# A new stored order of all engines for a fused RWKV-6 attention and Fourier-mix block

## The chip, the cores and the metric

The kernel runs on one core of a Trainium2 chip. The metric is the device time of one execution in microseconds (us). Five engines work side by side, each through its own list of instructions, strictly in the order in which the list was written: TensorE (PE, matrix products; its weight loads are listed as PEld), VectorE (DVE), ScalarE (ACT), GpSimd (POOL) and SyncE (SP), which here only issues DMAs. An instruction waits on semaphores until the instructions it depends on have ended; everything behind it on the same engine waits with it.

## The reference

The first half is a linear attention with a state that decays by step; the second mixes its output by a two-dimensional Fourier transform and puts it through a small two-layer network.

```python
# r, k, v, w: (4 batches, 8 heads, 768 steps, 48); u: (8, 48)
for t in range(S):
    cur = einsum('bhd,bhe->bhde', u * k[t], v[t])
    y[t] = einsum('bhd,bhde->bhe', r[t], state + cur)
    state = w[t][..., None] * state + einsum('bhd,bhe->bhde', k[t], v[t])
x = y as (4, 768, 384)
mixed = real(fft over d of (fft over t of x))
u = x + mixed
un = (u - mean) / sqrt(var + 1e-6)             # over the 384
out = u + relu(un @ w_ch1) @ w_ch2              # 384 -> 1536 -> 384
```

## The kernel before

**Tiling.** Each batch's 768 steps are six chunks of 128 steps on the partitions, so there are 24 chunks; the text writes (b, c) for chunk c of batch b. For each chunk four loads of 192 KB bring w, k, r and v (`load_one`, L621, issued at L624 on SP) into rings of seven buffers a name (`NIN`, L482). `attention` (L783) takes the logarithm of w on ScalarE, sums it over the steps by a matmul with a mask (L799; where the variant `sum_two` is taken also one with the other mask, L822), turns the sums into exponentials, multiplies r and k with them into `rkh`, transposes these (on TensorE at L899 or L911, or by a DMA transpose, L889), multiplies them into the score matrix (L922), masks it on VectorE (L932), updates the state (L954 to L963, from v in bf16, `vb`) and forms the output of the chunk (L984, L987). `fold` (L1014) adds and subtracts mirrored columns, and `mix` (L1048) does the Fourier transform as matmuls with cosine and sine tables (L1063 to L1068, then L1107 or L1116), adds, normalizes, transposes (L1203, or by DMA, L1210) and runs the network by halves of a batch: the first layer is 12 groups of three matmuls (L1235) a half, the second three outputs of 12 matmuls (L1254). So the network of batch b is done while the attention of batch b+1 is under way, and the network of the last batch has nothing beside it. The network's weights come by three DMAs from the POOL queue (`weights`, L766; issued at L769 twice for the first matrix and at L774 for the second); the first has to wait for a load of batch 0 (`W_AFTER`, L31).

**Variants.** Many steps have several forms with the same result (`choose`, L168): an eviction or a product on one engine or two, a transpose by TensorE or by DMA. Which form is taken, and which engine does a step that two engines could do, is decided by the numbers that stand in the stored order.

**The order.** `ORDER` (L38) holds, for each of the five engines, the numbers of the operations in the order in which the engine gets them. Nothing is sorted when the kernel is built; `schedule` (L227) walks the five lists with a model of the durations, and out of this come only the PSUM bank of every tile and some extra waits: a reused bank waits for its former tile, and an operation of POOL waits for the last operation of VectorE that the model put ahead of it on the port they share:

```python
for t, (_, i) in zip(o.opens, free):
    t.bank = i
    if bank[i] is not None:
        o.deps |= set(bank[i].ops)
```

The model's price for a load is the `xfer` in `load_one`, 998 ns for every load. Operations 2638 to 2669 are 32 matmuls without any use (`warm`, L1320): they are placed in the TensorE list like others and keep this engine active. The 16 matmuls at L1287 at the start serve the same end.

**What the steps ahead touch.** The list "sp" with the loads, the transposes at L889 and L1210 and the outputs at L1274; the list "pe"; the place of the three weight DMAs in the list "pool"; `load_one`.

Of the kernel before, what the change touches and what calls it, by code (L numbers as in the profile page):

```python
# [65 lines left out]
    "act": (  # L66
# [384 lines left out]
def bass_rwkv6_finch__then__fnet_fourier_mix_kernel(  # L451
# [169 lines left out]
    def load_one(b, c, n):  # L621
        was, g.ctx = g.ctx, ("load", b, c, n)
        i = (b * NC + c) % NIN
# [731 lines left out]
```

## Time and profile before

| | us |
|---|---|
| median of 3 runs | 182.34 (182.21 to 183.43) |
| the profiled execution, its own time | 182.32 |
| its span, first to last instruction | 180.2 |
| TensorE busy | 172.6 |
| VectorE, ScalarE, GpSimd busy | 155.7, 130.2, 111.0 |

The span is what the views of the profile show; 2.1 us of the execution's time lie around it. A busy TensorE is counted from the issue of a matmul to its modelled end, so matmuls that overlap in the pipeline are one stretch; for sums the distance between the starts of two successive matmuls is the better measure. A wait in the profile is put down to whatever released it last. The granted clock of TensorE stands in a row of its own.

### The profile page before, as it was taken

The page shows a single profiled execution, that of the slowest core. Times are in us where ns is not written, and L with a number is a line of the kernel's source. Part 1 is how long each engine was busy: PE and PEld are TensorE (multiplying, and loading weights), DVE is VectorE, ACT ScalarE, POOL GpSimd, SP SyncE. Part 2 cuts the span into 40 slices and gives each one's busy share as a digit, 9 for nine tenths or more (in the row PEclk, how much of TensorE's full clock was granted, in tenths as well). Part 3 has the DMA queues.
Part 4 walks back from the last instruction along what each step waited for, and adds up shares of the span by engine and source line. Part 5 has one row for each costly group of instructions (what it writes and reads, how often), then busy time and mean ns, then how long its engine had stood idle before and what let it go on. Part 6 is the DMA issues. An engine that isn't in the chain of part 4 may idle for free.

```text
span 180.2 us, 4569 instructions
## 1 busy us (share of the span) xinstructions
PE 172.6 (96%) x1704; PEld 113.9 (63%) x1704; DVE 155.7 (86%) x372; ACT 130.2 (72%) x311; POOL 111.0 (62%) x140
## 2 busy tenths in 40 slices
PE   5988899999999999999999999999999999999994
PEld 2455566766666576866676766665666776656663
DVE  7699999779998899999999999799999966882543
ACT  3989979589899686899997994986981754290500
POOL 2437779697464588599899865898988070310000
PEclk9999999999999999999999999999999999999999
DMA  5999998998998989999899999999973213304113
GB/s 118 209 209 204 178 200 169 183 208 163 171 206 173 211 166 241 202 204 210 191 216 187 232 161 210 233 160 196 217 162 51 91 44 63 135 4 100 39 58 131
DMA packets 117303, 29.29 MB, mean 163 GB/s; under 512 B 112545, under 2 KB 117282, under 8 KB 117282
## 3 DMA queue, kind: packets, MB, share of 16 engines
q1 hardware_dynamic: 115698, 26.65, 73.5%
q0 software_dynamic: 1584, 2.36, 7.7%
q8 instruction: 13, 0.21, 0.5%
q14 instruction: 8, 0.07, 0.1%
HBM read 23.59 MB, written 4.72 MB: 157 GB/s over the span
## 4 chain that ended last, share of the span: by engine, by line
PE 78%; DVE 7%; DMA 5%; ACT 4%; SPq 2%; issue 2%; POOL 1%; DVEq 0%; POOLq 0%; ACTq 0%
PE bank L1254 23%; PE bank L1235 23%; PE bank L1107 4%; PE bank L922 3%; PE bank L1063 3%; DMA in_v<-in_v_dram 3%; PE bank L911 3%; PE bank L1321 2%; PE bank L987 2%; DMA in_w<-in_w_dram 2%; PE bank L799 2%; PE bank L984 2%; PE bank L959 2%; SPq L889 1%; DVE ah L932 1%
## 5 line engine op out<-in xcount | busy, mean ns | idle before, releaser
L1254 PE MATMUL bank<-w,ht 128*128 128x384 bf16 (+2 forms) x300 | 52.8, 319 | 0.0
L1235 PE MATMUL bank<-unt,w 128*128 128x384 bf16 x288 | 52.0, 326 | 0.0
L1243 ACT ACTIVATE ht<-bank 128x384 bf16<-128x384 f32 x70 | 31.2, 497 | 13.2 <-PE bank L1235 13.0
L1254 PEld LDWEIGHTS bank<-w,ht 128*128 128x128 bf16 x300 | 27.5, 98 | 15.4
L1235 PEld LDWEIGHTS bank<-unt,w 128*128 128x128 bf16 x288 | 27.0, 98 | 15.7 <-DVE ah L932 0.2
L932 DVE TENSOR_TENSOR ah<-bank,msk 128x512 bf16<-128x512 f32 x42 | 27.4, 682 | 0.2 <-PE bank L922 0.2
L578 POOL TENSOR_TENSOR rkh<-in_k,e 128x384 bf16<-128x384 f32 x19 | 19.0, 1002 | 7.2 <-ACT e L840 4.9
L1263 DVE SCALAR_TENSOR_TENSOR osb<-bank,rstd,uf 128x384 f32<-128x384 f32 (+2 forms) x25 | 14.7, 596 | 9.0 <-PE bank L1254 9.0
L578 POOL TENSOR_TENSOR vtd<-in_v,dc 128x384 f32<-128x384 f32 x22 | 18.1, 830 | 5.7 <-DVE rk L578 4.1
L578 POOL TENSOR_TENSOR rk<-in_r,in_k 128x384 f32<-128x384 f32 x18 | 17.9, 1001 | 0.0
L578 POOL TENSOR_TENSOR rk<-rk,ub 128x384 f32<-128x384 f32 x17 | 16.9, 997 | 0.8 <-DVE rk L578 0.5
L1241 DVE TENSOR_SCALAR ht<-bank 128x384 bf16<-128x384 f32 x26 | 13.7, 547 | 2.9 <-PE bank L1235 2.9
L601 ACT ACTIVATE rkt<-bank 128x512 bf16<-128x512 bf16 (+1 forms) x19 | 14.5, 781 | 1.1 <-PE bank L911 1.1
L592 ACT ACTIVATE lb<-in_w 128x384 bf16<-128x384 f32 x24 | 12.3, 521 | 3.0 <-DMA in_w<-in_w_dram 2.9
L592 ACT ACTIVATE vb<-in_v 128x384 bf16<-128x384 f32 x23 | 11.9, 522 | 2.2 <-DMA in_v<-in_v_dram 2.2
L578 POOL TENSOR_TENSOR xf<-sd 128x384 bf16<-128x384 f32 (+1 forms) x9 | 8.9, 999 | 7.4 <-DVE xf L578 5.0
L871 DVE TENSOR_REDUCE dc<-rk 128x8 f32<-128x384 f32 (+1 forms) x24 | 12.5, 526 | 0.1
L853 DVE TENSOR_TENSOR rkh<-bank,in_r 128x384 bf16<-128x384 f32 x21 | 11.5, 547 | 0.4 <-ACT bank L852 0.4
L998 DVE TENSOR_TENSOR x<-bank,vtd 128x384 f32<-128x384 f32 x21 | 11.4, 549 | 0.2 <-POOL vtd L578 0.2
L826 ACT ACTIVATE e<-bank 128x392 f32<-128x392 f32 (+1 forms) x18 | 8.8, 497 | 3.4 <-PE bank L813 2.6
L852 ACT ACTIVATE bank<-bank 128x384 f32<-128x384 f32 x21 | 10.1, 486 | 1.7 <-PE bank L799 1.6
L987 PE MATMUL bank<-vb,ah 128*128 128x48 bf16 x192 | 11.1, 183 | 0.0
(185 smaller groups left out, 373.2 us busy)
## 6 DMA issues: line engine op xcount, KB each, us to landing
in_w<-in_w_dram SPq DMA_DIRECT2D x24, 192.0 KB, 3.8
in_r<-in_r_dram SPq DMA_DIRECT2D x24, 192.0 KB, 3.8
in_k<-in_k_dram SPq DMA_DIRECT2D x24, 192.0 KB, 3.9
in_v<-in_v_dram SPq DMA_DIRECT2D x24, 192.0 KB, 4.0
out_dram<-osb SPq DMA_DIRECT2D x23, 192.0 KB, 2.8
w<-in_moe_w_ch_dram POOLq DMA_DIRECT2D x2, 576.0 KB, 8.6
w<-in_moe_w_ch_dram POOLq DMA_DIRECT2D x1, 1152.0 KB, 11.1
out_dram<-osb SPq DMA_DIRECT2D x1, 128.0 KB, 1.7
```

The source lines that it names most:

```text
L578: return lambda e: e.tensor_tensor(out=o, in0=a, in1=b, op=f)
L592: return lambda e: e.activation(o, a, f, **kw)
L601: {"act": lambda e: e.activation(o(), i(), ACTF.Copy), "dve": lambda e: e.tensor_copy(out=o(), in_=i())}, **kw)
L853: op("dve", v_1(DM), lambda e: e.tensor_tensor(out=rh[:, :, 0:D], in0=ps(tce)[:, 0:DM].rearrange("t (h d) -> t h d", d=D), in1=rt[:, :, :] ...
L871: op("dve", v_1(H * m), lambda e: e.tensor_reduce(out=dc[:, :], in_=rku[:, :, 0:m], axis=mybir.AxisListType.X, op=ALU.add), r=[("RK", i2)] ...
L932: masked[n].append(op("dve", v_1(512), lambda e: e.tensor_tensor(out=ah[:, x:H:2, :], in0=ps(bk)[:, :].rearrange("p (h t) -> p h t", t=128 ...
L987: ins = e.matmul(ps(ty)[:, D * h:D * h + D], ah[:, h, :], vb[:, h, :], start=first and not ype, stop=True, skip_group_check=True)
L1235: ins = e.matmul(ps(t)[:, 0:384], W1[:, m, 256 * (j // 2) + j % 2:256 * (j // 2) + 256:2], unt[:, :, m, :], start=(m == 0), stop=(m == NM ...
L1241: {"dve": lambda e, j=j, t=t, ht=ht: e.tensor_scalar(out=ht[:, j, :], in0=ps(t)[:, 0:384], scalar1=su, scalar2=0.0, op0=ALU.mult, op1=ALU. ...
L1243: "act": lambda e, j=j, t=t, ht=ht: e.activation(ht[:, j, :], ps(t)[:, 0:384], ACTF.Relu, scale=su)},
L1254: ins = e.matmul(ps(t)[:, 0:hi - lo], ht[:, j, 128 * x:128 * x + 128], W2[:, j, lo:hi], start=(j == 0), stop=(j == NJ - 1))
L1263: op("dve", v_1(hi - lo) + 64, lambda e: e.scalar_tensor_tensor(out=o[:, lo:hi], in0=ps(t)[:, 0:hi - lo], scalar=rstd[:, kb:kb + 1], in1=u ...
```

## The change

All five lists of `ORDER` are replaced, and the model's price of a load becomes 1040 ns in batch 2 and 1075 ns in batch 3. Compared by the operations' numbers, the two orders differ in this:

- 1418 operations stand in both. 73 are dropped and 78 are new, all of them other forms of the same steps: one DMA transpose of `rkh` fewer (chunk (3, 1) is transposed on TensorE now, in one tile), `sum_two` instead of other forms in chunks (3, 2) and (3, 4), transposes of `rkh` in two tiles instead of one or the reverse in nine chunks, and sixteen single choices of other steps.
- TensorE gets 1714 matmuls instead of 1704: two more at L822 and eight more transposes.
- 117 operations that stand in both orders change their engine, in all directions between ScalarE, VectorE and GpSimd.
- The useless matmuls stay 32. Before, four of them stand ahead of the product at L660; now seven do. The last six stand around the Fourier transform of batch 1 in both.
- The loads come in another sequence. Counted without the small load of u: w of chunk (1, 0) is 27th instead of 26th; r of (1, 0) is 33rd instead of 31st and v of (1, 0) 31st instead of 33rd; w of (3, 2) moves from 95th to 91st, v of (3, 5), the last load of all before, from 116th to 99th.
- On POOL, between operation 338 (a product of chunk (0, 4)) and the first weight DMA (434) there stood 7 operations, 372 395 425 424 342 311 399, and there stand 9 now, 401 383 372 371 424 342 395 312 425.

The diff, cut to the first rows of the list "pe", to those rows of "pool" and of "sp" that the text speaks of, and to the load's price:

```diff
 ORDER = {
     "pe": (
-        "7 2638 2639 2640 2641 72 98 100 153 101 154 68 151 66 64 123 125 2642 180 181 130 206 183 137 204 "
...
+        "7 2638 2639 2640 2641 2642 2643 2644 72 100 68 101 98 151 153 2645 154 66 64 2646 127 180 128 259 "
...
     "pool": (
-        "1 3 2 4 40 37 51 46 35 44 171 175 120 173 41 226 228 275 371 279 310 309 344 321 338 372 395 425 424 "
-        "342 311 399 434 312 435 450 666 643 49 660 696 662 772 713 436 749 664 50 48 717 784 787 825 802 770 "
...
+        "3 4 1 2 36 51 52 43 47 37 169 42 120 173 133 226 281 309 344 321 338 401 383 372 371 424 342 395 312 "
+        "425 434 666 435 772 643 696 660 713 665 662 436 765 766 717 784 664 689 742 802 819 877 823 883 929 "
...
     "sp": (
-        "77 70 75 71 74 79 78 81 83 82 80 76 84 85 86 87 89 92 88 91 90 94 95 93 96 690 637 692 743 691 638 "
-        "639 744 640 745 796 693 798 797 856 855 854 746 912 913 911 799 914 857 1356 1303 1409 589 1304 1305 "
...
+        "81 75 70 79 74 71 77 78 85 82 83 76 80 87 89 84 86 91 88 90 92 690 93 94 95 638 743 637 96 692 691 "
+        "640 744 639 745 796 693 746 797 798 854 856 855 799 912 913 911 857 1356 914 1303 589 1358 1409 1304 "
...
@@ load_one
-               w=[("in", n, i)], sem="in_%s%d" % (n, i), xfer=998)
+               w=[("in", n, i)], sem="in_%s%d" % (n, i),
+               xfer=998 if b < 2 else 1040 if b < 3 else 1075)
```

In the list "sp", 637 to 640 are w, k, r and v of chunk (1, 0), 743 to 746 those of (1, 2), 693 is v of (1, 1).

127 rows, old and new, of the table ORDER are left out of this document.

## The prediction

> **What bounds the kernel now.** I read the page first (busy time, clock, chain), then the busy time by stretches.
>
> ```profile
> span 180.2 us, 4569 instructions
> PE 172.6 (96%) x1704; PEld 113.9 (63%) x1704; DVE 155.7 (86%) x372; ACT 130.2 (72%) x311; POOL 111.0 (62%) x140
> PEclk9999999999999999999999999999999999999999
> PE 78%; DVE 7%; DMA 5%; ACT 4%; SPq 2%; issue 2%; POOL 1%; DVEq 0%; POOLq 0%; ACTq 0%
> ...
> L853 DVE TENSOR_TENSOR rkh<-bank,in_r 128x384 bf16<-128x384 f32 x21 | 11.5, 547 | 0.4 <-ACT bank L852 0.4
> ```
>
> ```profile
> core 0: us, PE busy (x) PEld busy (x) DVE busy (x) ACT busy (x) POOL busy (x), PEclk, DMA share, GB/s
> 10.00:30.00 20.00, 17.95 (x232) 11.76 (x232) 19.77 (x42) 17.39 (x36) 14.69 (x20) 1.00 0.98 192
> 30.00:100.00 70.00, 69.99 (x773) 48.12 (x772) 65.58 (x149) 60.50 (x147) 53.81 (x63) 1.00 1.01 195
> 110.00:120.00 10.00, 9.28 (x100) 6.59 (x95) 8.74 (x23) 7.29 (x18) 8.95 (x10) 1.00 1.06 204
> 120.00:130.00 10.00, 9.73 (x92) 6.00 (x91) 9.58 (x21) 8.08 (x22) 8.91 (x10) 1.00 1.20 213
> 130.00:154.00 24.00, 24.00 (x215) 16.28 (x213) 20.64 (x54) 12.96 (x36) 12.53 (x16) 1.00 0.36 80
> ```
>
> TensorE bounds it, at full clock in every slice, without a hole from 30 to 100 us and from 130 us on. It has holes in three places: before 30 us, at 110 to 120 and at 120 to 130. In all three the DMA share is about 1.0 or above it: there TensorE waits for loads. The chain of waits names them and gives the spacing of the big groups:
>
> ```profile
> 69.91 0.33 PE bank L922 x8
> ...
> 88.96 0.22 PE bank L911 x4
> ...
> 108.73 3.62 DMA in_w<-in_w_dram
> 112.38 0.53 ACT lb L592
> 113.05 0.32 PE bank L799
> ...
> 118.20 4.62 DMA in_v<-in_v_dram
> 122.84 0.53 ACT vb L592
> 123.37 0.39 ACT st L601
> 123.80 0.34 PE bank L959 x4
> ...
> 160.04 5.85 PE bank L1254 x36
> 165.89 5.85 PE bank L1235 x36
> 171.74 5.89 PE bank L1254 x48
> ```
>
> 36 matmuls take 5.85 us, so one of 384 columns takes 0.162 us; a transpose of four blocks takes 0.22, a score matrix 0.33. With such spacings for every TensorE operation I add up the **queued work**: what stands ahead of an operation in the stored order, counted from TensorE's first matmul at 1.90 us. The rows of the timeline are that matmul and the mask matmuls of chunks (1, 0) and (3, 3).
>
> ```profile
> 1.90 4.78 PE L1287 MATMUL bank<-w 128*128 128x384 bf16 x16 [1.90 <-DVE w L589]
> ...
> 30.40 0.33 PE L799 MATMUL bank<-lb,msk 128*128 128x384 bf16 x1
> ...
> 110.90 0.33 PE L799 MATMUL bank<-lb,msk 128*128 128x384 bf16 x1
> ```
>
> The start of an operation minus 1.90 and minus its queued work is its **lag**, the time that TensorE has lost until then. With 1.90 included, the queue reaches the mask matmul of (1, 0) at 26.1 (it starts at 30.40: lag 4.3), that of (3, 3) at 105.3 (110.90: 5.6), that of (3, 2) at 106.6 (113.05: 6.4), the state of (3, 3) at 116.9 (123.80: 6.9), and its own end at 170.5 (171.74 + 5.89 = 177.6: 7.1). Hence span = 170.5 + 7.1 + 2.6 of tail = 180.2, and the execution's 182.32 is 2.1 more; the median is 182.34, so no correction is needed.
>
> **The change, part by part.**
>
> *Work.* Two more matmuls at L822 (2 x 0.162) and eight more transposes (two groups of 0.22) make 0.77 us: the queue ends at 171.3. The useless matmuls stay 32, so nothing is won or lost there. What changes engine or form on the others, at the mean durations of its groups in this trace, adds 0.3 us to VectorE and 0.2 to ScalarE and takes 1.3 from GpSimd. I cost that at nothing: TensorE hides it. Where VectorE is full (19.77 of 20 us before 30 us) this cover is thin: at 547 ns a product (the L853 row), one product too many ahead of a critical one costs 0.5 us there. I keep 0.5 us to either side for it.
>
> *The new price of a load* moves no byte. It reaches the chip only through the PSUM banks and the waits on VectorE's last operation that the model hands out. A bank wait costs between 0 and one more eviction of some 0.5 us; as 30 to 100 us shows no hole with the old hand-out, I take 0 and keep 0.5.
>
> *Loads ahead of 30 us.* The load of w(1, 0) is 27th instead of 26th. The rows are SP's issues, the 25th and 26th load merged in the first, the 27th in the second; behind them stand the times to landing of the issues at 24.4 (the 26th), 25.55 and 31.88.
>
> ```profile
> 23.33 2.18 SPq L624 DMA_DIRECT2D in_w<-in_w_dram  x2
> 25.55 0.70 SPq L624 DMA_DIRECT2D in_r<-in_r_dram  x1
> ...
> 30.82 1.02 SPq L624 DMA_DIRECT2D in_k<-in_k_dram  x1
> 31.88 1.02 SPq L624 DMA_DIRECT2D in_v<-in_v_dram  x1
> ```
>
> ```profile
> in_w<-in_w_dram SPq DMA_DIRECT2D x1, 192.0 KB, 3.8
> in_r<-in_r_dram SPq DMA_DIRECT2D x1, 192.0 KB, 4.6
> in_v<-in_v_dram SPq DMA_DIRECT2D x1, 192.0 KB, 11.7
> ```
>
> The 26th landed at 24.4 + 3.8 = 28.2, the 27th at 25.55 + 4.6 = 30.2. As w(1, 0) it may land anywhere from 28.9 (one fast load later) to 30.2; add the 0.53 us logarithm and 0.14 to the matmul as at 112.38 to 113.05. TensorE's new queue asks for it at 25.6, so the lag there becomes 4.0 to 5.3, against 4.3. I take 5.0: it is behind v(0, 5) too, now 28th instead of 24th, which the output of (0, 5) needs (queue 26.8).
>
> *Batch 3.* w(3, 2) is 91st instead of 95th load or store; two DMA transposes stood ahead of it, one stands behind now and one is gone. It lands about 4 us earlier, and the queue asks for it at about the same place: the stall at 113 us goes (6.4 − 5.6 = 0.8 us). v(3, 3) loses one transpose and one store ahead of it and gets the load of v(3, 5): it lands 0 to 1.5 us earlier. The state of (3, 3) stands at 117.4 in the queue. At the old landing the lag there is 123.37 − 117.4 = 6.0 (the 0.39 us of `st` stood between them on ScalarE by chance of the order), so that this stall of 0.4 shrinks or goes.
>
> What is late next is the transpose of batch 2's first half:
>
> ```profile
> L1210 SPq DMA_TRANSPOSE unt<-un x1: 1363/1363/1363, 119.8 to 119.8; - x1
> ...
> DMA to landing us min/median/max: 4.2/4.2/4.2
> ```
>
> It landed at 119.8 + 4.2 = 124.0. The network of batch 2 stands at 117.7 in the new queue: lag 6.3 if it lands as before, 5.7 if it gains half of a transpose. The last Fourier product ahead of it stands 1.7 us later in the queue (111.4 instead of 109.7), which at the same lag of about 6 less the 0.8 us stall means some 0.8 us later: 7.1 as the upper end.
>
> *Sum.* The early lag of 5.0 plus what crept in between 30 and 110 us before (5.6 − 4.3 = 1.3) gives 6.3; the late gate gives 5.7 to 7.1. I take 6.3. Span = 171.3 + 6.3 + 2.6 = 180.2; with 2.1 the time is **182.3 us**: 0.8 us of stalls goes, 0.8 us of work comes. Own range: lag 5.3 to 7.4 gives 181.3 to 183.4.
>
> **The rivals.**
>
> *A load is caught behind the weights (slower).* In the trace v(1, 0), issued 31.88, took 11.7 us, while k of (1, 2), issued 1.06 us earlier, came through normally. Between them the first weight DMA is issued, on POOL:
>
> ```profile
> 30.30 0.60 POOL L578 TENSOR_TENSOR xf<-x 128x192 bf16<-128x192 f32 x1
> 30.85 0.83 POOL L578 TENSOR_TENSOR vtd<-in_v,dc 128x384 f32<-128x384 f32 x1
> 31.62 0.97 POOL L769 DMA_DIRECT2D w<-in_moe_w_ch_dram  x1
> ```
>
> ```profile
> q0 software_dynamic: 761, 1.13, 83.5%
> q1 hardware_dynamic: 1921, 0.36, 27.8%
> ```
>
> From 34 to 42 us the weights' queue holds the engines (83.5%) and the loads get 27.8%. A load issued 0.26 us behind the weights was caught, one 0.80 ahead of them was not. The 33rd load was v(1, 0), whose product had time until 44.0 in the queue; now it is r(1, 0), and its transposes stand at 34.5, about 39.5 us. If r lands at 43.5, TensorE is free at 43.5 + 0.55 product + 0.2 = 44.3: 4.8 us lost. The lag at the end is then 5.0 + 4.8 and up to 1.1 of creep, 9.8 to 10.9 instead of 6.3: 185.8 to 186.9 us. Against it: POOL has nine operations ahead of the weights instead of seven, 6.8 instead of 5.0 us at 0.6, 0.83 and 1.0 us each, so that they are issued at 32.4 to 33.4, 0.5 to 1.5 us behind r. The rival decides from a lead under 0.8 us on, and the sequence of issues may shift by as much. A smaller case of the same: v(1, 1), the 36th load, is now asked for at 44.9 instead of 47.8, while the second matrix moves up on POOL; 3 us if it is caught. Together 0.25.
>
> The Trainium skill ("DMA: Bandwidth & Descriptors", Queues, rings and completion order) says that each DMA engine takes turns between its queues packet by packet. By that a caught load would get every second turn, land near 39 us, and this rival would cost next to nothing. The trace speaks against it: 11.7 us.
>
> *Another wait takes the place (slower by 2 to 3 us).* The DMA transposes of chunks (3, 2) and (3, 3) still stand ahead of v(3, 3) on SP, and SP waits at each until VectorE and GpSimd have made r and k of the chunk; behind it wait v(3, 3), the transpose of batch 2 and r and k of (3, 4). If VectorE's new list puts four products more ahead of these (4 x 0.547 = 2.2 us), the late gate opens 2.2 us later, at 184.5. VectorE has 8.74 busy of 10 us there, which speaks for room; chance 0.07.
>
> *All gates open (faster).* w(1, 0) lands at 28.9, nothing creeps in, the transpose gains 1 us: lag 4.5 to 5, span 178.4 to 178.9, 180.5 to 181.0. The part of it below 180.5 gets 0.14; the 30 to 100 us row, already without a hole, speaks against more.
>
> *The change does not do what it says.* A charge for thin activity can only pay where the clock falls, and PEclk is 9 in all 40 slices; this gives the forecast's time and lies in its share.
>
> The Trainium skill ("TensorE: Matmul & The Clock Gate", Part 1) says that an idle window of about 3.4 us halves the clock. The longest hole in the chain here is the 0.8 us at 113 us and the clock stays 1.00, so that no run here shows it; an estimate from that page is 1.7 us more in the first rival, 188.
>
> **How the numbers follow.** The forecast has 0.54, the slower rivals 0.32, the faster one 0.14. A measurement of this kernel can tell about 1% (1.8 us) from no change, so these are the three chances. The range is 180.6 to 186.4: below it lies the faster rival (0.14), above it the worse quarter of the caught load (0.06).
>
> **What would show it.** Right: TensorE's x1714; no wait at L799 near 113 us; a wait for `unt` or `in_v` near 123 us of under 1 us; a queue that starts the last layer (36 matmuls at L1254, then 36 at L1235 and 48, in whatever mixture) within 1 us of before. r(1, 0) landing near 36 us clears the first rival; a TensorE hole of 3 to 5 us between 39 and 50 us with `in_r` or `in_v` as its releaser proves it. PEclk under 9 anywhere would show that the useless matmuls stand wrongly. Wrong altogether would be holes between 50 and 100 us, where I found no reason for one.

## The result and the profile after

The changed kernel takes 184.03 us (median of 10 runs, 183.41 to 188.76), the kernel before beside it 182.47 us (10 runs): a ratio of 1.0078, 95% interval 1.0052 to 1.0103. It is slower by 0.8%, 1.6 us, inside the range that I gave and on the other side of my 182.3. The profiled execution took 183.94 us at a span of 182.1, 1.9 us more than before. Of the 1.9 us the time shows 1.6, since 1.8 us lie around the span now and not the 2.1 that I had added; why, I don't know.

First the page of the changed kernel (span, busy time, granted clock by slice, chain).

```profile
span 182.1 us, 4588 instructions
...
PE 175.0 (96%) x1714; PEld 115.5 (63%) x1714; DVE 157.0 (86%) x381; ACT 130.0 (71%) x310; POOL 110.0 (60%) x136
...
PEclk9997899999999999999999999999999999999999
...
PE 80%; DVE 16%; issue 3%; ACT 1%; DVEq 0%; ACTq 0%
```

The x1714 is as counted. The clock row isn't what I had foreseen: slices 4 and 5 show 7 and 8. The stretches of the changed kernel (columns as in the prediction: us, PE, PEld, DVE, ACT, POOL, granted clock, DMA share, GB/s), with two of 3.42 us around the dip:

```profile
10.00:30.00 20.00, 17.97 (x217) 11.58 (x217) 18.95 (x43) 16.91 (x36) 12.46 (x16) 0.91 1.01 197
30.00:100.00 70.00, 69.97 (x777) 48.02 (x773) 65.48 (x151) 60.69 (x147) 54.53 (x61) 1.00 0.97 191
110.00:120.00 10.00, 10.00 (x105) 7.11 (x104) 9.74 (x24) 8.11 (x19) 7.79 (x9) 1.00 1.07 194
120.00:130.00 10.00, 9.73 (x105) 5.97 (x102) 10.00 (x25) 8.12 (x21) 8.57 (x11) 1.00 0.97 185
130.00:154.00 24.00, 24.00 (x214) 16.38 (x213) 20.98 (x51) 14.87 (x41) 12.27 (x16) 1.00 0.39 85
12.88:16.30 3.42, 2.54 (x36) 1.41 (x35) 3.40 (x7) 3.10 (x6) 1.45 (x2) 1.00 1.09 216
16.30:19.72 3.42, 3.19 (x22) 1.89 (x23) 2.51 (x6) 2.33 (x7) 2.11 (x3) 0.50 1.01 196
```

The stall at 113 us is gone (10.00 of 10 instead of 9.28). From 16.3 to 19.7 us TensorE runs at half its clock. From 120 us on TensorE's busy column looks as before, 9.73 and 24.00 in both; VectorE has no room left from 120 to 130 us (10.00 of 10 instead of 9.58).

Where the 1.9 us arise shows in one operation, the score matrices of the last chunk (3, 5). They are the timeline's group of 16 matmuls reading `rkt` at 133.43 before and at 135.50 after, two groups of eight. In the trace the group of (3, 5) starts at 133.66 before and at 135.73 after, and from there to the end of the span it is 46.5 us before and 46.4 after. In every kernel of this study it is 46.4 to 46.5. So **everything is decided ahead of the scores of (3, 5)**. First the row of the kernel before, then of the changed one:

```profile
133.43 0.62 PE L922 MATMUL bank<-rkt 48*128 48x128 bf16 x16
```

```profile
135.50 0.62 PE L924 MATMUL bank<-rkt 48*128 48x128 bf16 x16
```

By the prediction's count the first matmul comes 0.27 us later (2.17 instead of 1.90), the queue is 0.77 us longer, and the lag is about 1 us higher at the end: 6.2 instead of 4.7 at output (0, 5) (33 us), 7.4 at 94 us, 8.3 at the end instead of 7.3. (Counted again, the kernel before has a queue of 170.3 and a lag of 7.3 at the end, where the prediction has 170.5 and 7.1; the sum is the same 177.6.)

### The profile page after: what moved, and what is told of

Its sections match the earlier page's. It is cut to its first block, busy times and chain, and to the rows that moved or that the text cites. A ratio compares the mean times of both kernels' runs of the same rounds, so it can differ in the third digit from the quotient of the medians.

```text
span 182.1 us, 4588 instructions
## 1 busy us (share of the span) xinstructions
PE 175.0 (96%) x1714; PEld 115.5 (63%) x1714; DVE 157.0 (86%) x381; ACT 130.0 (71%) x310; POOL 110.0 (60%) x136
## 4 chain that ended last, share of the span: by engine, by line
PE 80%; DVE 16%; issue 3%; ACT 1%; DVEq 0%; ACTq 0%
PE bank L1237 26%; PE bank L1256 24%; PE bank L1109 4%; PE bank L924 3%; DVE ah L934 3%; PE bank L1065 2%; PE bank L801 2%; PE bank L901 2%; PE bank L1323 2%; PE bank L989 2%; PE bank L986 2%; PE bank L913 2%; DVE rk L579 2%; PE bank L961 2%; DVE rkh L855 1%
## 5 line engine op out<-in xcount | busy, mean ns | idle before, releaser
L579 POOL TENSOR_TENSOR rk<-rk,ub 128x384 f32<-128x384 f32 x20 | 19.7, 1000 | 5.4 <-DVE rk L579 2.9
L579 POOL TENSOR_TENSOR rkh<-in_k,e 128x384 bf16<-128x384 f32 x18 | 18.0, 1002 | 5.9 <-ACT rkt L602 2.6
L579 POOL TENSOR_TENSOR vtd<-in_v,dc 128x384 f32<-128x384 f32 x20 | 16.5, 830 | 6.1 <-DVE rk L579 2.5
L579 POOL TENSOR_TENSOR rk<-in_r,in_k 128x384 f32<-128x384 f32 x17 | 17.0, 1001 | 2.9 <-DVE rkh L579 2.6
L855 DVE TENSOR_TENSOR rkh<-bank,in_r 128x384 bf16<-128x384 f32 x23 | 12.5, 549 | 1.1 <-ACT bank L854 0.9
L854 ACT ACTIVATE bank<-bank 128x384 f32<-128x384 f32 x23 | 11.2, 486 | 2.6 <-PE bank L801 2.4
L828 ACT ACTIVATE e<-bank 128x392 f32<-128x392 f32 (+1 forms) x20 | 9.7, 496 | 4.5 <-PE bank L815 3.9
L579 POOL TENSOR_TENSOR xf<-sd 128x382 bf16<-128x382 f32 (+1 forms) x7 | 7.0, 1002 | 9.2 <-DVE xf L579 6.8
L579 POOL TENSOR_TENSOR sd<-x 128x385 f32<-128x385 f32 x10 | 9.9, 1009 | 2.3 <-DVE x L1000 2.2
L593 ACT ACTIVATE vb<-in_v 128x384 bf16<-128x384 f32 x21 | 10.8, 524 | 0.7 <-DMA in_v<-in_v_dram 0.7
```

The source lines that it names most:

```text
L579: return lambda e: e.tensor_tensor(out=o, in0=a, in1=b, op=f)
L593: return lambda e: e.activation(o, a, f, **kw)
L855: op("dve", v_1(DM), lambda e: e.tensor_tensor(out=rh[:, :, 0:D], in0=ps(tce)[:, 0:DM].rearrange("t (h d) -> t h d", d=D), in1=rt[:, :, :] ...
```

## The experiments

Two theories of the early part stand against each other: the extra lag ahead of 33 us decides the end (A), or a gate in batches 2 and 3 does (B). Lags are by the prediction's count.

**Old and new halves.** The stored order was put together from both kernels, cut at 31 us of the old and 33 us of the new one; and the load queue alone was exchanged. The expectations speak of its first 58 entries; the kernels that ran exchange the first 21, loads of batch 0, and leave v(0, 5) and the loads of batch 1 in their places.

```diff
 loads_before: the changed kernel
     "sp": (
-        "81 75 70 79 74 71 77 78 85 82 83 76 80 87 89 84 86 91 88 90 92 690 93 94 95 638 743 637 96 692 691 "
+        "77 70 75 71 74 79 78 81 83 82 80 76 84 85 86 87 89 92 88 91 90 690 93 94 95 638 743 637 96 692 691 640 "
...
 loads_after: the kernel before, its first 21 entries the other way round
 early_before: the changed kernel, so exchanged in all five lists
     "pe": (
-        "7 2638 2639 2640 2641 2642 2643 2644 72 100 68 101 98 151 153 2645 154 66 64 2646 127 180 128 259 "
+        "7 2638 2639 2640 2641 72 98 100 153 101 154 68 151 66 64 123 125 2642 180 181 130 206 183 137 204 "
...
 early_after: the kernel before, the other way round
```

> The changed kernel, with everything that the kernel before started in its first 31 us (all five engines, its loads, its choices of form) put back in its old order, and the new order behind it. The TensorE work is that of the changed kernel. Theory A (the 1.5 us of lag that the changed kernel has gathered by 33 us is the loss, and nothing later takes it up): lag at output (0,5) back from 6.2 to about 4.7, the 0.26 us of the later first matmul back too, so 184.0 - 1.5 - 0.3 = about 182.3. Theory B (the end is set late, by the transposes through DMA of batches 2 and 3, whatever the early lag): about 184.0, with the lag that is saved early lost again at 122 to 126 us.

> The counterpart: the changed kernel's first 33 us, and behind them the order, forms and choices of the kernel before; the TensorE work is 0.77 us less than the changed kernel's. Theory A: the kernel before's 182.5 + 1.5 + 0.3 = about 184.3 if the extra lag stays to the end, or about 183.5 if the 0.8 us stall at 113 us (the load of w(3,2)) is swallowed by it. Theory B: about 182.5.

> The changed kernel with only its first 58 entries of the load queue put back in the order of before; the lists of the four other engines are the new ones. Theory A1 (the early lag comes from the order of the loads: w(0,2) first, w(0,1) and v(0,1), v(0,2) and v(0,5) later): lag at output (0,5) down by 1 us or more, 182.4 to 183.0. Theory A2 (it comes from the lists of VectorE and ScalarE, which wait for the data in the new sequence): no gain, 184.0 or longer, since the lists now ask for data in another sequence than they come.

> The kernel before with only the first 58 entries of its load queue in the new sequence. Theory A1: lag at output (0,5) up from 4.7 by 1 us or more, 183.5 or longer. Theory A2: about 182.5.

Measured: 185.31, 186.51, 186.31 and 186.17 us beside 182.60, ratios 1.0150 (1.0081 to 1.0219), 1.0220 (1.0142 to 1.0297), 1.0203 (1.0130 to 1.0275) and 1.0165 (1.0084 to 1.0245). The two halves miss both theories. They brought delays of their own where they were joined (1.8 us at 33 us in early_before; 3.2 us at 33 to 39 us in early_after, a dip of the clock from 35.9 to 39.3 us among them), so they say nothing on A and B. The load queue belongs to the lists around it: exchanged alone it raises the lag at output (0, 5) to 7.7 and 9.5 (the second in the slowest execution, with two dips). By their times loads_before fits A2 and loads_after A1, so these two decide nothing on the loads either, and nothing on v(0, 5), which they leave where it was.

One thing early_after shows all the same. Its first 33 us are the changed kernel's, list for list, yet its lag at output (0, 5) is 5.1 and not 6.2. The stretches of early_after around 16.3 us:

```profile
12.88:16.30 3.42, 2.50 (x35) 1.39 (x35) 3.40 (x7) 3.10 (x6) 1.49 (x2) 1.00 1.10 216
16.30:19.72 3.42, 3.22 (x34) 2.21 (x35) 3.42 (x9) 3.25 (x9) 2.07 (x3) 1.00 1.03 206
```

From 9 to 16 us TensorE's matmuls in the two traces start within 0.05 us of each other; at 20 us, behind the dip, the changed kernel's are 1.3 us later, and from 24 to 32 us 1.0 us. At a full clock 34 matmuls were issued in the second stretch, at half the clock 22. So the **clock** (theory C: it costs; theory D: it lies beside waits for VectorE) became a suspect.

**Four causes alone.**

```diff
 fill_gap: the changed kernel, six useless matmuls moved in "pe" (of 25 to 32 us)
-        "... 180 128 259 181 130 206 183 207 137 204 147 ..."
+        "... 180 128 259 2647 2648 2649 2650 181 130 206 2651 183 207 137 2652 204 147 ..."
 w1x_first: the changed kernel, "dve"
-        "41 49 45 39 28 6 8 9 11 31 ..."
+        "6 41 49 45 39 28 8 9 11 31 ..."
 price: the kernel before
-               w=[("in", n, i)], sem="in_%s%d" % (n, i), xfer=998)
+               w=[("in", n, i)], sem="in_%s%d" % (n, i), xfer=998 if b < 2 else 1040 if b < 3 else 1075)
 w32_early: the kernel before, "sp" (2075 is w(3,2))
-        "... 627 634 2130 2186 2006 2059 2077 1243 2075 2129 ..."
+        "... 627 634 2075 2130 2186 2006 2059 2077 1243 2129 ..."
```

> The changed kernel with six of the useless matmuls that stand at 25 to 32 us put into TensorE's gaps at 13.3 (four), 15.0 and 16.1 us (one each); nothing else. Theory C (the stretch at half clock from 16.3 to 19.7 us is set off by the thin activity just before it, and costs 0.4 to 1.0 us): granted clock 1.00 in every execution, lag at output (0,5) down from 6.2 to 5.1 to 5.5, 183.0 to 183.6. Theory D (the dip is beside work that waits for VectorE anyway): 183.9 to 184.1 whatever the clock. If the gaps that are left at 25 to 32 us bring a dip there instead, the clock stays at 0.99.

> The changed kernel with the fill that the very first matmuls read put back from the sixth to the first place of VectorE's list. If TensorE's start is what the end hangs on: first matmul at about 1.5 to 1.9 instead of 2.17 and 183.5 to 183.8. If VectorE's chain of batch 0 sets the pace (its work is the same, only in another sequence): 184.0, the head gained lost again by 9 us.

> The kernel before with the new transfer prices of batches 2 and 3 alone, its own stored order kept: the prices only reach the hand-out of PSUM banks, in which 145 of 293 tiles (from 75.9 us on) get another bank. Theory E (banks come free long before they are wanted): 182.5, and a lag from 76 us on as before, within 0.2. Theory F (a bank handed out by a wrong forecast makes TensorE wait for an eviction): 0.3 to 1 us longer.

> The kernel before with only the load of w(3,2) moved six places ahead in the load queue, before r(3,3); its slot has been free since 67 us. Theory G (a stall that goes in the middle is a gain at the end, nothing later takes it up): the 0.74 us stall at 113 us gone, lag at the mask matmul of (3,2) 5.7 instead of 6.4, 181.7. Theory B (the transposes through DMA at 120 to 124 us set the end): lag at state (3,3) still 6.9 to 7.1 and 182.4.

- fill_gap: 186.33 us, ratio 1.0240 (1.0193 to 1.0286). The clock stayed full and the lag at output (0, 5) fell to 4.8, and then 1.7 us were lost at one place. TensorE's row of fill_gap, VectorE's and GpSimd's beside it, and VectorE's same operation in the changed kernel:

```profile
40.14 0.34 PE L1106 MATMUL bank<-dtm,hcr 128*128 128x384 bf16 x1 [1.68 <-DVE hcr L580]
```

```profile
37.78 2.30 DVE L580 TENSOR_SCALAR hcr<-hcs,cp 128x384 bf16<-128x384 bf16 x1
```

```profile
38.01 1.94 POOL L576 TENSOR_TENSOR rk<-in_r,in_k 128x384 f32<-128x384 f32 x2
```

```profile
38.51 0.32 DVE L583 TENSOR_SCALAR hcr<-hcs,cp 128x384 bf16<-128x384 bf16 x1
```

  A VectorE operation of 0.32 us took 2.30 us while GpSimd worked, which it did without a gap from 37.05 to 39.95 us. The plan orders such pairs by waits (`last` in `schedule`); moving six matmuls in the stored order had changed which of the two goes first. The experiment was spoiled by that and had to be made again.
- w1x_first: 183.82 us, ratio 1.0094 (1.0063 to 1.0125). The first matmul starts at 1.32 instead of 2.17, and the gain is lost in a wait for ScalarE's logarithm, so that the matmul at L824 (here L821) starts at 8.91 as it did at 8.92. The later head of the changed kernel costs nothing up to there. The time itself says little of it, since all six executions have a granted clock of 0.99, with a dip from 11.0 us on in the trace.

```profile
1.32 4.18 PE L1286 MATMUL bank<-w 128*128 128x384 bf16 x16 [1.32 <-DVE w L587]
...
8.91 0.32 PE L821 MATMUL bank<-lb,nle 128*128 128x384 bf16 x1 [1.01 <-ACT lb L590]
```

- price: 182.44 us, ratio 1.0023 (0.9995 to 1.0052). No loss clear of the noise, as theory E has it; but the interval reaches 0.9 us, so that this run alone doesn't exclude the smaller losses of theory F. In its trace TensorE's matmuls run 0.3 us behind the kernel before from 10 us on, 0.8 us from 94 to 120 us and 0.3 us again from 124 us on: a delay of 0.5 us that is taken up.
- w32_early: 181.53 us, ratio 0.9970 (0.9934 to 1.0007). The stretch from 110 to 120 us has 10.00 of 10 instead of 9.28, the stall of 0.72 us is gone and the time is 0.7 us less, as theory G had it, though the interval just reaches 1.

**The clock, without the side effect.** The useless matmuls were now moved in TensorE's own list alone, behind the planning, so that banks and waits stay as they were.

```diff
+    every = list(g.ops)
     g.schedule(ORDER)
+    g.order["pe"] = [every[int(i)] for i in PE_EMIT.split()]
     g.emit()
 PE_EMIT of fill_gap_emit: the list "pe" of fill_gap
 PE_EMIT of warm_ahead: the list "pe" of before, but
-    "7 2638 2639 2640 2641 72 98 100 ..."
+    "7 2638 2639 2640 2641 2642 2643 2644 2645 2646 72 98 100 ..."
```

> The same six useless matmuls moved into the gaps at 13.3 to 16.1 us, but only in the list that TensorE is given: banks, and the waits of GpSimd for VectorE that the plan works out from the stored order, stay those of the changed kernel, so that the 2.30 us that one VectorE operation (0.32 us in the changed kernel) took at 37.8 us behind two GpSimd additions should go. Theory C: granted clock 1.00, lag at output (0,5) 4.8 to 5.1 instead of 6.2 and no jump behind it: 182.6 to 183.2. Theory D: 183.9 to 184.1. If the jump at 38 us comes back (lag 7.3 at 40 us), it isn't the plan's order between the two engines that makes it.

> The kernel before, with five of its useless matmuls (those at 11.9, 19.8, 21.1, 23.4 and 23.6 us) given to TensorE at 7.2 us, ahead of the correction's sums, as the changed kernel does with three; its plan is kept. Theory C: stretches at half clock between 13 and 27 us in some executions (0.99 or less) and 182.5 to 183.2. Theory D: 182.2 to 182.5, since TensorE waits for VectorE there.

fill_gap_emit: 183.22 us, ratio 1.0053 (1.0026 to 1.0079), a full clock in all ten executions, lag 4.9 at output (0, 5), no jump behind it. warm_ahead: 184.35 us, ratio 1.0091 (1.0050 to 1.0132), a dip in all ten. Theory C holds in both directions, though warm_ahead came out 1.2 us above its expected range. In its trace the same matmuls start 1.0 us later than in the kernel before at 10 us already, ahead of the dip, which fits the five matmuls given early (5 x 0.162 us and a wait), and 2.5 us later at 20 us, behind it. The kernel before gives the price of a dip too: over its 108 executions beside the experiments, 13 had a granted clock of about 0.99, with a median of 183.6 us, and 95 one of about 1.00, with 182.3: **1.3 us for one dip**.

**Work taken out of the middle.** Six useless matmuls of 76 to 85 us, where TensorE waits for nothing, were moved into the early gaps, where it waits anyway.

```diff
 fill_late: the changed kernel, PE_EMIT as above, but the six are those of 76 to 85 us
 w32_fill: w32_early, PE_EMIT, three of the six behind 206, one behind 137, two behind 320
```

> The changed kernel with the six useless matmuls that stand at 76 to 85 us (6 x 0.163 = 0.98 us, in a stretch where TensorE waits for nothing) put into the gaps at 13.3 (four), 15.0 and 16.1 us, in TensorE's own list alone. If TensorE's work behind 33 us counts one for one at the end (the rule by which the forecast priced the 0.77 us of added work): clock 1.00 and 183.2 (the run with the other six moved) - 0.98 = 182.2, queue end at 170.2, lag as there (7.6 at 135 us). If the transposes through DMA of batches 2 and 3 set the end: 183.0 to 183.2, the lag at 125 us a good half microsecond higher than there.

> The kernel before with the load of w(3,2) six places ahead, and its six useless matmuls of 76 to 84 us put into the gaps at 13.4 (three), 14.8 (one) and 21.4 us (two), in TensorE's own list alone. By the rule above: 182.3 - 0.65 - 0.98 = 180.7, and no execution at a clock of 0.99. If a wait stands behind each of the six, which only covers it: 181.6.

fill_late: 183.32 us, ratio 1.0042 (1.0016 to 1.0068). w32_fill: 181.56 us, ratio 0.9943 (0.9912 to 0.9973). The clock was full in both, and the kernels are as fast as fill_gap_emit and w32_early. For fill_late that is no test, since fill_gap_emit has had six matmuls taken out as well, those of 25 to 32 us, so that the rule itself would have the two level. The traces decide. w32_fill is 0.22 us ahead of w32_early in the same matmuls at 74 us and 0.22 at 86 us; fill_late is 0.60 and 0.75 us ahead of after_side (the changed kernel at a full clock, below). So of the 0.98 us nothing and 0.15 us are left as early as 86 us: the six had covered delays that came up in their place, though TensorE had shown no gap there. The rule "one for one" fell, and B came back. w32_fill is the one version whose interval lies wholly below 1: 0.6% faster than the kernel before.

**What the rest is.** Three more single causes.

```diff
 more_work: the kernel before
...
+    late.fn = lambda e: [one(e) for _ in range(6)][-1]
 undo_price: fill_gap_emit
-               xfer=998 if b < 2 else 1040 if b < 3 else 1075)
+               xfer=998)
 undo_tr31: fill_gap_emit; 2056 to 2058 (TensorE, TensorE, ScalarE) go, "sp":
-        "... 2078 2075 1257 2006 2130 2129 ..."
+        "... 2078 2075 1257 2006 2059 2130 2129 ..."
```

> The kernel before, with the useless matmul at 40.2 us issued six times instead of once (5 x 0.162 = 0.81 us more for TensorE, plan and all other lists unchanged). If TensorE's work counts one for one: 182.3 + 0.8 = 183.1, lag unchanged beside it. If gates at 76 to 84 us (VectorE busy 9.7 of 10 us) and at 112 to 124 us (loads, transposes through DMA) set the end: 182.3 to 182.6, the stall at 113 us and the wait at 123 us shrinking by what was added.

> The changed kernel with its early gaps filled (183.2), and the transfer price of the loads put back to 998 in all batches: stored order the same, banks and GpSimd's waits for VectorE handed out by the old price. If the hand-out is part of the remaining 0.9 us: 182.7 or less; if not: 183.1 to 183.4.

> The changed kernel with its early gaps filled (183.2), and the transposes of chunk (3,1) put back from TensorE to the DMA queue, behind that of (3,0), as before: two groups of four transposes (0.45 us) and an eviction less, one DMA transpose more ahead of r(3,3) and r(3,2). If the added work is what remains: 182.75. If the late gates are: 183.2, or up to 1 us longer where the transpose holds the loads behind it back (w(3,2) and v(3,2) stand ahead of it).

more_work: 183.03 us, ratio 1.0019 (0.9982 to 1.0057), undecided between 0 and 0.8 us. undo_price: 183.47 us, ratio 1.0065 (1.0042 to 1.0087): the price isn't what remains. undo_tr31: 183.95 us, ratio 1.0075 (1.0049 to 1.0102): with 0.45 us of work less its median is 0.7 us above that of fill_gap_emit, and about 1 us is lost at 111 us in its trace, where TensorE stands idle for 0.99 us ahead of a score matrix. The transposes that the change gives to TensorE are no loss.

**Side by side.** The changed kernel, the filled one, and one with two more useless matmuls given ahead.

```diff
 after_side: the changed kernel
 fill_side: fill_gap_emit
 after_thin: the changed kernel, PE_EMIT:
-    "... 2643 2644 72 100 68 101 98 151 153 2645 154 66 64 2646 127 ..."
+    "... 2643 2644 2645 2646 72 100 68 101 98 151 153 154 66 64 127 ..."
```

> The changed kernel itself, timed beside the next two on one chip. 184.0; some executions at a granted clock of 0.99, some at 1.00, these 0.4 us faster (by the ten executions of before) or up to 1.6 us faster (if a dip costs here what it costs in the kernel before).

> The changed kernel with its gaps of 13.3 to 16.1 us filled by six useless matmuls from 25 to 32 us, once more, beside it. Theory C: clock 1.00 in all executions and 0.6 to 0.9 us under after_side. Theory D: within 0.2 us of after_side's executions at a full clock.

> The changed kernel with its two useless matmuls of 10.1 and 11.9 us given to TensorE at 7.8 us as well, so that the stretch from 10 to 16 us is thinner still. Theory C: a dip in all executions (0.99 or less), 184.2 to 185.0. Theory D: 184.0 as after_side.

after_side: 183.89 us, ratio 1.0091 (1.0057 to 1.0125); fill_side: 183.26 us, ratio 1.0044 (1.0019 to 1.0069); after_thin: 184.22 us, ratio 1.0116 (1.0080 to 1.0152), with a dip in three of its six and not in all, as expected. Of 15 executions of the changed kernel (those shown at the top and these, without the one of 188.76 us) 7 had a dip (median 184.1) and 8 had none (183.7): the dip costs 0.4 us here, and filling the gaps brings some 0.5 us more than the clock. Where these come from isn't shown. In the traces v(0, 5), the load that the forecast names, landed at 31.77 in after_side and at 30.06 in fill_side, and only the first has a wait for it (ScalarE's `vb` is v in bf16):

```profile
31.80 0.52 ACT L593 ACTIVATE vb<-in_v 128x384 bf16<-128x384 f32 x1 [0.90 <-DMA in_v<-in_v_dram]
```

```profile
32.37 0.22 PE L986 MATMUL bank<-st,rkt 128*128 128x96 bf16 x1 [0.32 <-ACT vb L593]
```

The profiled execution of after_side had a full clock, and its span is 182.1 all the same. That is the key to the rest. Its lag at output (0, 5) is 5.6 instead of 6.2, at 111 us 6.8 instead of 7.4; at the scores of (3, 5) it is 8.1, with the dip 8.2. The same matmuls start 0.7 us later with the dip from 60 to 132 us, and 0.1 us later from these scores on. TensorE's rows of after_side there:

```profile
134.81 0.40 PE L924 MATMUL bank<-rkt 48*128 48x128 bf16 x8
135.64 0.40 PE L924 MATMUL bank<-rkt 48*128 48x128 bf16 x8 [0.43 <-ACT xf L1046]
```

The profile names ScalarE's `xf` as the releaser, which ended at 135.60. But in w32_fill, where no such operation ends nearby, it names the DMA transpose of `rkh`:

```profile
133.49 0.40 PE L949 MATMUL bank<-rkt 48*128 48x128 bf16 x8 [0.16 <-DMA rkt<-rkh]
```

I set the landing of that transpose beside the start of the scores for every kernel (times in us, from the traces):

| kernel | transpose of (3, 5) issued | landed | scores of (3, 5) start | span |
|---|---|---|---|---|
| before | 129.36 | 132.44 | 133.66 | 180.2 |
| w32_early | 128.77 | 131.97 | 133.07 | 179.6 |
| w32_fill | 128.87 | 133.36 | 133.49 | 180.0 |
| changed (dip) | 131.54 | 135.44 | 135.73 | 182.1 |
| after_side (no dip) | 130.85 | 135.50 | 135.64 | 182.1 |
| w1x_first | 130.92 | 135.61 | 135.75 | 182.2 |
| after_thin | 131.29 | 135.84 | 135.98 | 182.4 |
| undo_tr31 | 130.80 | 135.17 | 135.30 | 181.7 |
| undo_price | 130.50 | 135.10 | 135.23 | 181.7 |
| fill_gap_emit | 130.83 | 134.97 | 135.11 | 181.5 |
| fill_late | 130.14 | 134.85 | 134.98 | 181.4 |
| fill_side | 130.26 | 134.29 | 134.46 | 180.9 |

In the seven rows from after_side to fill_late, and in w32_fill, the scores start 0.13 to 0.14 us behind the landing: **the transpose of (3, 5) is the gate**. fill_gap_emit and after_side show it with little else between them: from 60 to 132 us their matmuls start within 0.1 us of each other, the transposes are issued at 130.83 and 130.85, they land at 134.97 and 135.50, and the first kernel ends 0.5 us earlier. In the kernel before it had landed 1.2 us too early to matter. In the changed kernel with a dip, TensorE comes to the scores 0.29 us behind the landing, without a wait: there it is late by itself, and both ways end at 182.1. w32_fill has run into the gate too, its transpose having landed 1.4 us later than in w32_early.

What makes it late I looked for on two more engines. SyncE's queue of after_side, then of before, cut to what stands between the transpose of batch 2's first half and those of chunks (3, 4) and (3, 5):

```profile
121.17 1.30 SPq L1212 DMA_TRANSPOSE unt<-un  x1
122.52 0.58 SPq L625 DMA_DIRECT2D in_r<-in_r_dram  x1
123.14 0.64 SPq L625 DMA_DIRECT2D in_k<-in_k_dram  x1
123.83 0.84 SPq L1276 DMA_DIRECT2D out_dram<-osb  x1
124.71 0.43 SPq L625 DMA_DIRECT2D in_k<-in_k_dram  x1
125.18 0.68 SPq L1276 DMA_DIRECT2D out_dram<-osb  x1
125.91 0.43 SPq L625 DMA_DIRECT2D in_r<-in_r_dram  x1
...
129.24 2.84 SPq L891 DMA_TRANSPOSE rkt<-rkh  x2
```

```profile
119.79 1.36 SPq L1210 DMA_TRANSPOSE unt<-un  x1
...
122.50 1.04 SPq L624 DMA_DIRECT2D in_r<-in_r_dram  x1
123.59 0.78 SPq L624 DMA_DIRECT2D in_k<-in_k_dram  x1
...
127.44 3.15 SPq L889 DMA_TRANSPOSE rkt<-rkh  x2
```

The transpose of batch 2 is issued 1.4 us later, and in the new list two stores stand ahead of r(3, 5): its load is issued at 125.91 instead of 122.50. Yet the loads aren't what the transpose waited for: k(3, 5) had landed at 128.00 and r(3, 5) at 129.43, and their products start at 129.77 on GpSimd and at 130.02 on VectorE, both engines having worked without a gap up to there. The product of k with the decay that the transpose needs is GpSimd's. First after_side, then before:

```profile
123.83 1.61 POOL L579 TENSOR_TENSOR vtd<-in_v,dc 128x384 f32<-128x384 f32 x2 [1.44 <-DVE un L584]
...
127.07 1.00 POOL L579 TENSOR_TENSOR rk<-in_r,in_k 128x384 f32<-128x384 f32 x1
128.02 1.01 POOL L579 TENSOR_TENSOR rkh<-in_k,e 128x384 bf16<-128x384 f32 x1
128.99 0.84 POOL L579 TENSOR_TENSOR vtd<-in_v,dc 128x384 f32<-128x384 f32 x1
129.77 1.01 POOL L579 TENSOR_TENSOR rkh<-in_k,e 128x384 bf16<-128x384 f32 x1
```

```profile
126.36 1.00 POOL L578 TENSOR_TENSOR rkh<-in_k,e 128x384 bf16<-128x384 f32 x1 [0.69 <-ACT e L840]
127.32 1.01 POOL L578 TENSOR_TENSOR rk<-in_r,in_k 128x384 f32<-128x384 f32 x1
128.28 1.00 POOL L578 TENSOR_TENSOR rkh<-in_k,e 128x384 bf16<-128x384 f32 x1
```

In both, the transpose is issued 0.07 us behind the end of the last row (130.78 and 129.28). In after_side GpSimd stood idle for 1.44 us until VectorE had done `un`, which `vtd` doesn't read (a wait that the plan adds between the two engines would fit), and then worked without a gap from 123.83 on, with another `vtd` ahead of the last product. It ends that product 1.5 us later. Then the transpose takes 4.7 us instead of 3.1 to land (SyncE's view of that one transpose, first after_side, then before):

```profile
DMA to landing us min/median/max: 4.7/4.7/4.7
```

```profile
DMA to landing us min/median/max: 3.1/3.1/3.1
```

So of the 3.06 us by which it lands later, 1.5 are a later issue and 1.6 a longer transfer. The longer transfer goes with a packet of another DMA queue, which the last section shows; that it is the cause, no run tested. A version with GpSimd's product ahead of `vtd` wasn't tried either.

## Why the prediction was wrong, step by step

- **Work, 0.77 us: the count right, its price not shown.** x1714 is as counted. But of 0.98 us less, at most 0.15 were left 2 us further on, 0.45 us less came with a loss in a third kernel, and 0.81 us more with an undecided 0.5 us. A term that I added one for one moves the end only where no wait stands behind it.
- **The new price, 0: right** within the noise, by price and undo_price.
- **Engine moves, 0 with 0.5 us to either side: partly wrong.** The head that came 0.27 us later is free (w1x_first). GpSimd's list in batch 3, which I only added up ("takes 1.3 from GpSimd"), holds the product on which the gate hangs, and its waits for VectorE.
- **The early gate, lag 5.0: a size off.** Measured 6.2 with a dip, 5.6 and 5.1 without. w(1, 0) landed at 30.0, at the upper end of my bounds, without a wait of TensorE for it. v(0, 5), which I had named beside it, does hold output (0, 5) up in after_side: it landed at 31.8, and TensorE stood 0.32 us. That TensorE waits for loads wherever the DMA share is 1.0 was read too quickly, though: from 10 to 30 us all its waits over 0.15 us in the kernel before are put down to VectorE and ScalarE. What I left out is the clock. I had read "PEclk is 9 in all 40 slices" off the old order and carried it over to the new one, in the rival "the change does not do what it says"; my own sign for that, a PEclk under 9, is there.
- **What creeps in from 30 to 110 us, 1.3: right** (6.2 to 7.5).
- **The stall at 113 us goes: right**, and worth its 0.7 us where nothing later takes it up (w32_early). The state of (3, 3): its load v(3, 3) landed 1.1 us later (123.9), not up to 1.5 us earlier.
- **The late gate, lag 5.7 to 7.1 with 6.3 taken: the step that failed.** At the scores of (3, 5) the lag is 8.1 to 8.2. I looked for one late gate, the transpose of batch 2's first half, which did land later (125.3 instead of 124.0). But TensorE loses its time elsewhere. From 122 to 126 us 0.8 us creep in with the dip, without it (after_side) and with filled gaps (fill_side) alike: in after_side the matmuls at 122.51 and 124.43 start 0.37 and 0.28 us later than the usual distance allows, behind VectorE's `uf` and `ah`. The lag there is 7.6 in after_side, above my upper end. The other 0.5 us of after_side is the gate that I didn't see, the transpose of (3, 5) behind GpSimd's list, with its longer transfer. What VectorE and GpSimd do I had costed at nothing since "TensorE hides it".
- **"A load is caught behind the weights": did not decide.** r(1, 0) was issued at 32.88 and landed at 36.4. v(1, 1) was caught, 10.8 us from 35.66 to 46.5, and TensorE has no wait over 0.15 us from 36 to 60 us. My rows for this rival were read too simply: 761 packets with 1.13 MB stand against 1921 with 0.36 MB, 1.5 KB each against 0.19, so that turns packet by packet needn't give a load half of the time, and 11.7 us doesn't speak against them.
- **"Another wait takes the place": right in kind**, but I gave it 0.07 and 184.5, since VectorE has room there. VectorE hasn't (10.00 of 10 from 120 to 130 us), the last product was GpSimd's, and the loads behind the transpose on SyncE, by which I had it come about, weren't waited for in after_side. The time came out half a microsecond below it.

With the measured sizes the sum closes: queue 171.3 with the later head (170.3, 0.27 and 0.77), lag 6.2 + 1.3 + 0.8 of waits from 122 to 126 us = 8.3, tail 2.5: 182.1. Of the 2 us between this lag and my 6.3, the early term has 1.2 and the late one the rest; at a full clock the late part has more (8.1 against 6.8 at 111 us).

## What to carry to other kernels

Look for the last operation behind which the remaining time is the same in both versions, and price a change by what releases that operation, slack included: of the 0.7 us by which a dip had delayed the matmuls ahead of the gate, the gate let 0.1 us through. Work that covers a wait is worth nothing either, even where the engine shows no gap. Follow each operand of the gate back to the engine that makes it, also on the engines that aren't the bound, with their waits for one another. A clock row read off one order says nothing of another, and filler belongs into the gaps.

## What the runs showed of the hardware

- **The clock can halve without a gap of one microsecond.** In the changed kernel TensorE was busy 2.54 of the 3.42 us ahead of the dip, its longest gap there was 0.64 us (for VectorE's `rkh`, at 13.65), and the clock then stood at 0.50 for 3.41 us; 7 of 15 executions had a mean clock of 0.99, as this one. With 2.23 us busy in the same stretch all ten executions of warm_ahead had one, and with 3.38, when the gaps were filled, none of fill_side's twelve. The stretches of loads_before, where it fell, and of fill_side:

```profile
12.88:16.30 3.42, 0.98 (x10) 0.55 (x9) 2.07 (x5) 1.41 (x3) 1.44 (x2) 1.00 1.11 220
16.30:19.72 3.42, 3.34 (x29) 1.83 (x30) 3.23 (x7) 3.11 (x8) 1.49 (x3) 0.56 1.01 199
```

```profile
12.88:16.30 3.42, 3.38 (x43) 1.79 (x41) 3.40 (x8) 3.08 (x7) 1.39 (x2) 1.00 1.10 217
16.30:19.72 3.42, 3.32 (x36) 2.21 (x35) 3.42 (x8) 3.25 (x9) 2.17 (x3) 1.00 1.07 212
```

  The changed kernel's trace has a second stretch at 0.50, from 183.54 us on, behind the end of the work: 49 times 3.413 us after the first at 16.29. The Trainium skill ("TensorE: Matmul & The Clock Gate", Part 1) has a window of about 3.4 us that runs freely, which fits this, the length of the dips and that the same lists dip in one execution and not in the next. It asks for an idle window; here a window three quarters busy was enough. Busy time alone doesn't draw the line: placed by the stretch at the end of each trace, windows with 0.92 to 2.55 us busy were followed by a dip, but windows with 2.44 to 2.52 in after_thin, early_after and early_before weren't. What is counted stays open.
- **VectorE stands still beside GpSimd.** 2.30 us instead of 0.32 us for the bfloat16 operation at 37.78 us in fill_gap, which ended 0.13 us behind GpSimd's two products. The Trainium skill ("SBUF — State Buffer", Who interferes with whom) calls the port pair of the two an exclusive lock; the trace agrees.
- **A DMA transpose takes longer beside an instruction packet.** The DMA queues from issue to landing of the transpose of (3, 5), in after_side and in the kernel before:

```profile
q1 hardware_dynamic: 2007, 0.73, 110.7%
q8 instruction: 1, 0.02, 1.4%
```

```profile
q1 hardware_dynamic: 1773, 0.60, 92.8%
```

  That one packet of 16 KB, of the kind "instruction", falls into this time in 14 of the 20 traces, and there the transpose took 3.9 to 4.7 us; in the six without it, 3.1 to 3.2 us. In the 14 the DMA queues moved under 20 GB/s for 0.8 to 1.6 us, from 0.4 to 0.9 us behind the packet's start; in the six for 0.5 us at most. In the kernel before the packet starts at 133.77, behind the landing, in after_side at 132.91. No run moved it alone, so the packet as the cause is likely and not shown.
